# Decays in front of a token taken as a reciprocal, in place of a second scan

## The chip, the core and the metric

The kernel runs on one core of a Trainium2 chip. The metric is the device time of one execution in microseconds, as a median of several runs. A core has five engines with a queue of instructions each: PE (TensorE, matmuls), DVE (VectorE), ACT (ScalarE), POOL (GpSimd) and SP (which here only starts transfers). They run side by side and wait for each other through semaphores.

## What is computed

A linear recurrence with decays (RWKV-6 attention) and, on its output, a mixture of 16 experts. For each of 4 batches and 8 heads, over 768 tokens of 48 channels:

```
state = 0                                   # 48 x 48
for t in range(768):
    y[t]  = r[t] @ (state + outer(u * k[t], v[t]))
    state = w[t][:, None] * state + outer(k[t], v[t])
x = y, with the heads of a token side by side        # 3072 x 384
g = argmax(x @ w_group);  e = argmax(x @ w_expert[g])
out = weight(g, e) * relu(x @ w1[g, e]) @ w2[g, e]   # F = 1024
```

The decays w lie between 0.8 and 0.95.

## The kernel before

It has two stages. In the first, the recurrence is worked out in blocks of 64 tokens (`C`); two heads form a pair, which fills the 128 partitions (48 channels each, padded to 64), and there are 16 pairs. In the second, the tokens of each expert are gathered and sent through its two weight matrices.

**Blocks.** Within a block, a state that comes in is multiplied by the decays up to a token, and what a token leaves behind is multiplied by the decays after it. So the kernel scales keys and queries once and does the rest by matmuls:

- `s` (line 323, in `suffixes`) holds for every token the product of its own decay and all later ones of its block. It is a scan on DVE, run backward over a row of 780: each block has 65 places, the first of which holds a decay of zero. A second operand, `first_of`, holds 1 at these places and `FLOOR` elsewhere; the scan takes the larger of the product and this operand, so that every block starts anew from 1 and no product falls below `FLOOR`.
- `kk` (line 328, POOL) is the keys times the decays after their token, which is `s` shifted by one place.
- `total` is the product over a whole block: 12 numbers in a partition.
- `e` (lines 342 to 347, `prefixes`) holds what a query is multiplied by: the decays from the beginning of the block up to just before its token, divided by `total`. DVE makes 12 reciprocals of `total` (line 344), puts them at the first places of the blocks in a tile `iv` that is zero elsewhere, and runs a second scan forward: at a block's first place the decay is zero and the reciprocal enters by addition, and from there on each place is the one before it times its decay.
- `q` (line 351, `queries`, DVE) is the queries times `e`.

The product of `q` and `kk` of two tokens in one block is then the product of the decays between them, since `total` cancels. `masked` takes these scores on PE (line 366), keeps the pairs in order of time (line 376, DVE), and puts the diagonal from a second set of scores (line 380, DVE). `growth` (line 402, PE) makes what each block adds to the state, `states` (line 412, DVE) carries the state from block to block by a scan, and `outer` (line 447, PE) applies it to `q`.

**Order of the work.** The order on PE, DVE, ACT and SP is written out by hand: each engine runs its instructions in the order in which the code calls for them. One call of `step(n)` serves pair n and prepares the next two. On DVE it gives, in this order: masking and diagonal of pair n (lines 376, 380); `prefixes` and `queries` of pair n+1; the carry scan of pair n (line 412); the backward scan of pair n+2 (line 323). Once in a batch the routing of a batch comes between them (lines 140 to 170 and 502 to 528), some fifteen small operations; line 170 there is a reciprocal of 6 elements. Before the first step, `suffixes`, `prefixes` and `queries` of pair 0 and `suffixes` of pair 1 are called alone. Some loads (lines 191 and 206 to 217) and some stores are issued only after a named operation, so that transfers don't crowd: among these operations are the results of `prefixes` and `queries`.

`s`, `iv` and the carry tiles have two buffers each, used in turn; `e` has one. The zeros in `iv` are set once, by DVE for one buffer (line 250) and by POOL for the other (line 301).

**Second stage.** For each of the 16 experts PE makes the hidden layer (line 852) and the output (lines 887 and 907), with small work on ACT and DVE, while the weights of the expert after next are loaded. The loads for the first two experts are cut into pieces and issued during the first stage.

If a decay lies outside 0.5 to 2.0, a slow loop over tokens computes everything anew at the end; with the inputs here it isn't run.

Of the kernel before, what the change touches and what calls it, by code (L numbers as in the profile page):

```python
# [35 lines left out]
F32 = mybir.dt.float32  # L36
# [3 lines left out]
ALU = mybir.AluOpType  # L40
# [4 lines left out]
C = 64  # L45
# [3 lines left out]
CAP = max(CAPS)  # L49
LOW, HIGH = 0.5, 2.0  # L50

FLOOR = 1e-30
AFTER = mybir.DependencyInfo(mybir.DependencyClass.Sync, mybir.DependencyReason.DATA)


# [1 line left out]
def rwkv_then_moe(  # L57
# [12 lines left out]
    nc = tc.nc  # L70
    B, HP, _, _, S = rk_d.shape
# [3 lines left out]
    WP = w_d.shape[3]  # L75
# [96 lines left out]
    with ExitStack() as first:  # L172
        ip = first.enter_context(tc.tile_pool(name="inputs", bufs=1))
# [24 lines left out]
        def load_pair(n, after=None):  # L198
            load(rks[n % NRK], rk_d[n // HP, n % HP], after)
# [26 lines left out]


        ss = [ip.tile([128, WP + 1], F32, name=f"s{i}", tag=f"s{i}") for i in range(2)]
        ivs = [ip.tile([128, WP], F32, name=f"iv{i}", tag=f"iv{i}") for i in range(2)]
        tots = [ip.tile([128, D, NB], F32, name=f"tot{i}", tag=f"tot{i}") for i in range(2)]  # L230
        gs = [ip.tile([128, D, NB], F32, name=f"g{i}", tag=f"g{i}") for i in range(2)]
        first_of = ip.tile([128, WP], F32, name="first_of", tag="first_of")
# [10 lines left out]
        nc.scalar.dma_start(out=u_sb, in_=u_d)  # L243
        nc.vector.memset(first_of, FLOOR)
        nc.vector.memset(first_of[:, 0:WP:C + 1], 1.0)
# [1 line left out]
        load_values(0)  # L247
        make_identity(nc, ident)
        load_pair(1)
        nc.vector.memset(ivs[0], 0.0)  # L250
        nc.scalar.dma_start(out=wr, in_=wp_d)
        make_upper_triangular(nc, ut, val=1.0, diag=False)

# [44 lines left out]
        id_i = const([128, NE], I32, "id_i")  # L298

        def rest_of_setup():  # L300
            nc.gpsimd.memset(ivs[1], 0.0)
            nc.gpsimd.memset(blank, 0.0)
            nc.gpsimd.memset(blank[:, DM:DM + 1].bitcast(I32), N)
            nc.gpsimd.memset(within, 1.0)
            nc.gpsimd.memset(within[:, :, 0:1], 0.0)
            nc.gpsimd.memset(ones, 1.0)
            nc.gpsimd.tensor_scalar(out=order[:, 0:SPLIT], in0=order[:, 0:SPLIT],
                                    scalar1=float(2 ** 20), scalar2=None, op0=ALU.add)
            for p in range(NE):
                if p == 0 or CAPS[p] != CAPS[p - 1]:  # L310
                    nc.gpsimd.memset(caps[:, p:], float(CAPS[p]))
# [5 lines left out]
        def blocked(a):  # L317
            return a.rearrange("p (n c) -> p n c", c=C)

        def suffixes(n):  # L320
            p = dict(n=n, hp=n % HP, rk=rks[n % NRK], w=ws[n % NW], v=vts[n % NV],
                     s=ss[n % 2], iv=ivs[n % 2], tot=tots[n % 2], g=gs[n % 2])
            p["scanned"] = nc.vector.tensor_tensor_scan(out=p["s"][:, 0:WP][:, ::-1], data0=p["w"][:, ::-1],  # L323
                                         data1=first_of[:, ::-1], initial=1.0,
                                         op0=ALU.mult, op1=ALU.max)
            p["total"] = p["s"][:, 0:WP].rearrange("p (n c) -> p n c", c=C + 1)[:, :, 1]
            kk = p["kk"] = p2.tile([128, S], F32, name="kk", tag="kk")
            p["made"] = nc.gpsimd.tensor_tensor(  # L328
                out=blocked(kk), in0=blocked(p["rk"][:, 1]), op=ALU.mult,
                in1=p["s"][:, 1:].rearrange("p (n c) -> p n c", c=C + 1)[:, :, 1:])  # L330
            return p
# [8 lines left out]
                           in_=p["total"][:, None, 1:].to_broadcast([128, D, NB - 1]))  # L340

        def prefixes(p):
            iv = p["iv"][:, 0:WP:C + 1]
            nc.vector.reciprocal(out=iv, in_=p["total"])
            p["e"] = p2.tile([128, WP], F32, name="e", tag="e", bufs=1)
            return nc.vector.tensor_tensor_scan(out=p["e"], data0=p["w"], data1=p["iv"], initial=0.0,  # L346
                                         op0=ALU.mult, op1=ALU.add)

        def queries(p):
            p["q"] = p2.tile([128, S], F32, name="q", tag="q", bufs=3)  # L350
            return nc.vector.tensor_tensor(
                out=blocked(p["q"]), in0=blocked(p["rk"][:, 0]), op=ALU.mult,
                in1=p["e"].rearrange("p (n c) -> p n c", c=C + 1)[:, :, 0:C])

        blocks = [(c, j, slice(C * (2 * c + j), C * (2 * c + j + 1)))
                  for c in range(NCH) for j in range(2)]
# [195 lines left out]
        for e in range(2):  # L552
            w1, w2 = weights[e] = expert_weights()
            for w, w_in in ((w1, w1_d[e]), (w2, w2_d[e])):
                w = w.rearrange("p c f -> p (c f)")
                q = w.shape[1] // 4
# [15 lines left out]
        def step(n):  # L572
# [21 lines left out]
            if z:  # L594
                loads.send(prefixes(z))
                at = queries(z)
# [26 lines left out]
            if n + 2 < TOTAL:  # L623
                pipe[n + 2] = suffixes(n + 2)
                at = pipe[n + 2]["scanned"]
# [4 lines left out]
        def outputs(n, p, y, b):  # L630
# [13 lines left out]
            if half == 1:  # L644
                turning.append((b, lgs.pop(b), xs[b]))

        p = pipe[0] = suffixes(0)
        scaled(p)
        prefixes(p)
        queries(p)  # L650
        with tc.issue_after(p["made"].ins):
            rest_of_setup()
        keys(p)
        totals(p)
        pipe[1] = suffixes(1)
        load_decays(2, pipe[1]["scanned"])
        load_pair(2, pipe[1]["scanned"])
# [44 lines left out]
        def in_order():  # L702
# [33 lines left out]
        n = TOTAL  # L736
        nc.vector.scalar_tensor_tensor(
            out=seen[:, 0:SPLIT], in0=base_of[:, 0:SPLIT], scalar=128.0, in1=seen[:, 0:SPLIT],
            op0=ALU.add, op1=ALU.max)
        early = [early_tile(e, first_slots(e), copy)  # L740
                 for e, copy in enumerate((nc.scalar.copy, nc.vector.tensor_copy))]
        y, p = pipe[n - 2], pipe[n - 1]
# [359 lines left out]
    with tc.If(n_any, preferred_fallthrough_block=False):  # L1102
        n_over = nc.values_load(count_i[0:1, 0:1], min_val=0, max_val=OVT,
                                skip_runtime_bounds_check_because="a count of the tiles in use")
        with tc.For_i(0, n_over) as i:
# [7 lines left out]
                              in_=w1_d[ds(ev, 1)].rearrange("o p f -> p (o f)"))  # L1113
            nc.sync.dma_start(out=w2.rearrange("p c d -> p (c d)"),
                              in_=w2_d[ds(ev, 1)].rearrange("o p f -> p (o f)"))
# [9 lines left out]
                out=xg, out_offset=None, in_=slot_dram,  # L1125
# [64 lines left out]
```

## Time and profile before

| | |
|---|---|
| median of 3 runs | 472.78 us (466.01 to 473.24) |
| profiled execution | span 464.2 us |
| busy: PE, DVE, ACT, POOL | 415.1, 217.3, 159.9, 121.2 us |
| first stage: last masking of scores begins | 153.2 us |
| second scan, line 346 | 16 times, 1783 ns each |
| backward scan, line 323 | 16 times, 1763 ns each |
| 12 reciprocals, line 344 | 16 times, 214 ns each |
| product for the queries, line 351 | 16 times, 1039 ns each |
| keys on POOL, line 328 | 16 times, 1776 ns each |

In a row of a group, the form is written as output and input (partitions x elements and type); after the count stand busy time and the mean of one in ns, then the idle time of the engine in front of it and what ended it. In a timeline, each line has start and duration in us, and in brackets the idle time before it with the releaser. In a table of windows, each line has the length of the stretch and each engine's busy time in it, with the number of instructions; the last three numbers are the clock granted to TensorE as a share of full speed, the share of time in which the transfer engines were busy, and GB/s. "issue" as a releaser means that the engine waited for nothing that the profile shows.

### The profile page before, as it was taken

The page shows a single profiled execution, that of the slowest core. Times are in us where ns is not written, and L with a number is a line of the kernel's source. Part 1 is how long each engine was busy: PE and PEld are TensorE (multiplying, and loading weights), DVE is VectorE, ACT ScalarE, POOL GpSimd, SP SyncE. Part 2 cuts the span into 40 slices and gives each one's busy share as a digit, 9 for nine tenths or more (in the row PEclk, how much of TensorE's full clock was granted, in tenths as well). Part 3 has the DMA queues.
Part 4 walks back from the last instruction along what each step waited for, and adds up shares of the span by engine and source line. Part 5 has one row for each costly group of instructions (what it writes and reads, how often), then busy time and mean ns, then how long its engine had stood idle before and what let it go on. Part 6 is the DMA issues. An engine that isn't in the chain of part 4 may idle for free. (4 is left out here: it accounts for less than half of the span.)

```text
span 464.2 us, 15159 instructions
## 1 busy us (share of the span) xinstructions
PE 415.1 (89%) x6682; PEld 351.3 (76%) x6682; DVE 217.3 (47%) x326; ACT 159.9 (34%) x372; POOL 121.2 (26%) x136
## 2 busy tenths in 40 slices
PE   1786878877787989999999999999999999999995
PEld 1775767657666778799798797897987977877882
DVE  8898889969997434115363462511111111111111
ACT  3675867746575622122031120220211211210220
POOL 6312111560281523211211320213130221221011
PEclk9998999989898979999999999999999999999999
DMA  6769666784783523587779879766665667675400
GB/s 236 262 174 280 192 202 182 232 310 134 236 279 122 165 70 111 186 298 258 279 236 349 317 280 356 264 218 213 214 243 215 198 243 256 215 275 201 155 24 25
DMA packets 28537, 101.03 MB, mean 218 GB/s; under 512 B 4071, under 2 KB 11332, under 8 KB 24880
## 3 DMA queue, kind: packets, MB, share of 16 engines
q1 hardware_dynamic: 23344, 86.13, 55.7%
q0 software_dynamic: 4832, 13.79, 8.0%
q8 instruction: 54, 0.88, 0.8%
q14 instruction: 19, 0.16, 0.1%
q10 hardware_dynamic: 288, 0.07, 0.1%
HBM read 85.50 MB, written 14.75 MB: 216 GB/s over the span
## 5 line engine op out<-in xcount | busy, mean ns | idle before, releaser
L852 PE MATMUL bank_a<-xt,w 128*128 128x208 f32 (+5 forms) x768 | 128.6, 327 | 0.9 <-DVE xt L865 0.9
L852 PEld LDWEIGHTS bank_a<-xt,w 128*128 128x128 f32 x768 | 124.0, 190 | 4.1 <-issue 3.0
L887 PE MATMUL bank_b<-w,ht 128*128 128x384 f32 x224 | 75.5, 490 | 0.0
L882 DVE TENSOR_SCALAR yo<-bank_b,xg 128x384 f32<-128x384 f32 (+5 forms) x30 | 16.1, 538 | 117.5 <-PE bank_b L887 64.6
L854 ACT ACTIVATE ht<-bank_a 128x208 f32<-128x208 f32 (+5 forms) x128 | 41.6, 326 | 80.5 <-PE bank_a L852 79.9
L887 PEld LDWEIGHTS bank_b<-w,ht 128*128 128x128 f32 x224 | 41.4, 190 | 26.5
L875 POOL DMA_INDIRECT out_dram<-yo,xg x30 | 28.8, 959 | 120.4 <-DVE yo L882 102.8
L907 PEld LDWEIGHTS bank_b<-w,ht 128*32 128x32 f32 (+1 forms) x1344 | 50.3, 107 | 9.9 <-issue 7.3
L907 PE MATMUL bank_b<-w,ht 128*32 128x96 f32 (+3 forms) x1344 | 57.2, 324 | 0.0
L114 POOL DMA_INDIRECT slot_scratch<-blank,behind x28 | 26.5, 946 | 100.9 <-DMA slot_scratch<-blank,behind 61.1
L328 POOL TENSOR_TENSOR kk<-rk,s 128x768 f32<-128x768 f32 x16 | 28.4, 1776 | 86.6 <-DVE s L323 34.0
L447 PE MATMUL y<-q,zs 64*48 64x64 f32 x704 | 27.9, 229 | 20.5 <-issue 16.6
L865 DVE COPY xt<-bank_b 128x384 f32<-128x384 f32 (+5 forms) x30 | 12.8, 464 | 70.6 <-PE bank_b L863 70.6
L447 PEld LDWEIGHTS y<-q,zs 64*48 64x48 f32 x704 | 24.4, 129 | 22.6 <-issue 18.4
L916 ACT COPY yo<-bank_b 32x96 f32<-32x96 f32 (+1 forms) x30 | 7.0, 232 | 90.7 <-DVE yo L882 90.5
L536 POOL DMA_INDIRECT slot_scratch<-x,dest x24 | 29.7, 1236 | 26.5 <-ACT q L688 10.8
L346 DVE TENSOR_TENSOR_SCAN e<-w,iv 128x780 f32<-128x780 f32 x16 | 28.5, 1783 | 0.5
L323 DVE TENSOR_TENSOR_SCAN s<-w,first_of 128x780 f32<-128x780 f32 x16 | 28.2, 1763 | 0.9 <-DMA w<-in_w_dram 0.9
L389 PE MATMUL bank<-ident,kk 128*128 128x128 f32 x96 | 16.3, 311 | 11.8 <-POOL kk L328 10.5
L421 ACT COPY zs<-ze 128x576 f32<-128x576 f32 x16 | 19.8, 1238 | 9.5 <-DVE ze L412 9.2
L455 ACT COPY xt<-y 128x768 f32<-128x768 f32 x16 | 12.8, 799 | 28.8 <-PE y L447 28.8
L389 PEld LDWEIGHTS bank<-ident,kk 128*128 128x128 f32 x96 | 11.8, 157 | 13.5 <-POOL kk L328 11.1
(170 smaller groups left out, 477.2 us busy)
## 6 DMA issues: line engine op xcount, KB each, us to landing
w<-in_w_dram SPq DMA_DIRECT2D x28, 1536.0 KB, 7.3
rk<-in_rk_dram SPq DMA_DIRECT2D x26, 384.0 KB, 4.2
wt<-in_w_dram SPq DMA_DIRECT2D x4, 1560.0 KB, 8.5
w<-in_w_dram SPq DMA_DIRECT2D x16, 384.0 KB, 4.3
w<-in_w_dram SPq DMA_DIRECT2D x26, 195.0 KB, 3.4
v<-in_v_dram SPq DMA_DIRECT2D x16, 288.0 KB, 4.3
xg<-slot_scratch SPq DMA_DIRECT2D x14, 193.0 KB, 6.2
rk<-in_rk_dram SPq DMA_DIRECT2D x3, 768.0 KB, 7.5
```

The costliest lines, as they stand in the source:

```text
L114: nc.gpsimd.indirect_dma_start(out=slot_dram, in_=blank[0:m], in_offset=None, out_offset=bass.IndirectOffsetOnAxis(ap=behind[0:m, p, i:i + ...
L323: p["scanned"] = nc.vector.tensor_tensor_scan(out=p["s"][:, 0:WP][:, ::-1], data0=p["w"][:, ::-1], data1=first_of[:, ::-1], initial=1.0, o ...
L328: p["made"] = nc.gpsimd.tensor_tensor(out=blocked(kk), in0=blocked(p["rk"][:, 1]), op=ALU.mult, in1=p["s"][:, 1:].rearrange("p (n c) -> p ...
L346: return nc.vector.tensor_tensor_scan(out=p["e"], data0=p["w"], data1=p["iv"], initial=0.0, op0=ALU.mult, op1=ALU.add)
L389: nc.tensor.transpose(b[:, c * 128:(c + 1) * 128], z[:, (c0 + c) * 128:(c0 + c + 1) * 128], ident)
L447: m = nc.tensor.matmul(p["y"][j][64 * t:64 * t + D, C * c:C * (c + 1)], lhsT=p["zs"][halves[t], i], rhs=p["q"][halves[t], C * i:C * (i + 1 ...
L536: m = nc.gpsimd.indirect_dma_start(out=slot_dram, out_offset=bass.IndirectOffsetOnAxis(ap=dest[:, c:c + 1], axis=0), in_=x[:, c, :], in_of ...
L852: nc.tensor.matmul(z[:, 0:n], lhsT=w1[:, dc, f * 128:(f + 1) * 128], rhs=xt[:, dc], start=(dc == 0), stop=(dc == DC - 1))
L854: nc.scalar.activation(out=ht[:, f, 0:n], in_=z[:, 0:n], func=AF.Relu)
L875: s = out_scatter[0] = nc.gpsimd.indirect_dma_start(out=out, out_offset=bass.IndirectOffsetOnAxis(ap=to, axis=0), in_=yo[0:m], in_offset=N ...
L887: nc.tensor.matmul(z[0:m, 0:DM], lhsT=ht[:, f, 0:m], rhs=w2[:, f], start=(f == 0), stop=(f == FC - 1))
L907: nc.tensor.matmul(z[32 * i:32 * i + k, c:c + b - a], lhsT=lhs, rhs=w2[:, f, a:b], start=(f == 0 and c == 0), stop=(f == FC - 1), skip_gro ...
```

## The change

The product of the decays up to just before a token, divided by the product over the whole block, is one over the product of the token's own decay and all later ones. That is what the backward scan holds at this token: with places counted as in a block of 65, `e[i] = 1 / s[i+1]`. So the change takes the reciprocal of `s` at all 64 tokens of each of the 12 blocks, 768 in a partition, and needs neither the second scan nor `iv`. It is meant to put one plain operation on DVE in place of a scan and a small operation. `e` loses the gaps between blocks in the part that is used, so that the product for the queries reads rows without gaps.

`FLOOR` goes from 1e-30 to 1e-20. It bounds the products from below, and so the reciprocals from above.

```diff
-FLOOR = 1e-30
+FLOOR = 1e-20
...
-        ivs = [ip.tile([128, WP], F32, name=f"iv{i}", tag=f"iv{i}") for i in range(2)]
...
-        nc.vector.memset(ivs[0], 0.0)
...
         def rest_of_setup():
-            nc.gpsimd.memset(ivs[1], 0.0)
...
         def prefixes(p):
-            iv = p["iv"][:, 0:WP:C + 1]
-            nc.vector.reciprocal(out=iv, in_=p["total"])
             p["e"] = p2.tile([128, WP], F32, name="e", tag="e", bufs=1)
-            return nc.vector.tensor_tensor_scan(out=p["e"], data0=p["w"], data1=p["iv"], initial=0.0,
-                                         op0=ALU.mult, op1=ALU.add)
+            return nc.vector.reciprocal(
+                out=blocked(p["e"][:, 0:S]),
+                in_=p["s"][:, 0:WP].rearrange("p (n c) -> p n c", c=C + 1)[:, :, 1:])
 
         def queries(p):
             p["q"] = p2.tile([128, S], F32, name="q", tag="q", bufs=3)
             return nc.vector.tensor_tensor(
-                out=blocked(p["q"]), in0=blocked(p["rk"][:, 0]), op=ALU.mult,
-                in1=p["e"].rearrange("p (n c) -> p n c", c=C + 1)[:, :, 0:C])
+                out=p["q"], in0=p["rk"][:, 0], in1=p["e"][:, 0:S], op=ALU.mult)
```

More of the change, by code (lines that the diff above doesn't have):

```diff
@@ L321, in suffixes @@
             p = dict(n=n, hp=n % HP, rk=rks[n % NRK], w=ws[n % NW], v=vts[n % NV],
-                     s=ss[n % 2], iv=ivs[n % 2], tot=tots[n % 2], g=gs[n % 2])
+                     s=ss[n % 2], tot=tots[n % 2], g=gs[n % 2])
             p["scanned"] = nc.vector.tensor_tensor_scan(out=p["s"][:, 0:WP][:, ::-1], data0=p["w"][:, ::-1],
```

## The prediction

> **What bounds the kernel now.** I read four views, from coarse to fine. First the page's busy shares and its 40 slices of 11.6 us, here the PE and DVE rows:
>
> ```profile
> PE 415.1 (89%) x6682; PEld 351.3 (76%) x6682; DVE 217.3 (47%) x326; ACT 159.9 (34%) x372; POOL 121.2 (26%) x136
> PE   1786878877787989999999999999999999999995
> DVE  8898889969997434115363462511111111111111
> ```
>
> The 89% of PE is an average over two stages. In the first 13 slices (to about 150 us) VectorE is mostly at 8 to 9 tenths and PE, after the first slice, at 6 to 8; later PE is at 9. The change lies wholly in the first stage, so PE's 89% says nothing on it.
>
> Second, the timeline of VectorE over one step of the first stage (start us, us, line):
>
> ```profile
> 36.62 0.93 DVE L376 TENSOR_TENSOR at<-scores,later 128x768 f32<-128x768 f32 x1
> 37.66 1.03 DVE L380 COPY_PREDICATED at<-diag_mask,scores 128x768 f32<-128x768 uint8 x1
> 38.58 0.22 DVE L344 RECIPROCAL iv<-s 128x12 f32<-128x12 f32 x1
> 38.84 1.78 DVE L346 TENSOR_TENSOR_SCAN e<-w,iv 128x780 f32<-128x780 f32 x1
> 40.65 0.96 DVE L351 TENSOR_TENSOR q<-rk,e 128x768 f32<-128x768 f32 x1
> 41.53 1.35 DVE L412 TENSOR_TENSOR_SCAN ze<-g,tot 128x576 f32<-128x576 f32 x1
> 42.80 1.75 DVE L323 TENSOR_TENSOR_SCAN s<-w,first_of 128x780 f32<-128x780 f32 x1
> 47.03 0.96 DVE L376 TENSOR_TENSOR at<-scores,later 128x768 f32<-128x768 f32 x1 [2.48 <-PE scores L366]
> ```
>
> The seven operations run back to back, 7.9 us from 36.62 to 44.55; only then does VectorE wait, 2.48 us, for PE's scores. Other steps have no bracket at L376: they begin at 20.95, 28.79 and 36.62, a period of 7.83 us that is VectorE's work alone. Third, all such waits:
>
> ```profile
> DVE at L376 <- PE scores L366: 11.2, 7, 3.9
> ```
>
> In 16 steps VectorE waits 11.2 us: 0.64, 2.48, 0.49, 1.26, 3.91, 1.86 and 0.59 by the timeline; nine steps have none. Fourth, two steps by windows (span, then PE, PEld, DVE, ACT, POOL):
>
> ```profile
> 28.79:36.62 7.83, 5.65 (x206) 4.82 (x205) 7.66 (x8) 5.91 (x11) 1.69 (x1) 1.00 0.62 155
> 36.62:47.03 10.41, 7.11 (x223) 6.10 (x216) 7.76 (x9) 5.20 (x10) 3.38 (x2) 0.84 0.94 295
> ```
>
> VectorE is busy 7.66 of 7.83 us in the first: it bounds the step. In the second its work is the same, and PE is late (granted clock 0.84, DMA share 0.94).
>
> [...]the trace of before has no large reciprocal. [...]the product q of 768 elements took 958 ns[...].
>
> **The change part by part.** *Reciprocal over 768 elements.* The two small reciprocals, and a neighbour of the same size (lines of the source view: min/median/max in ns):
>
> ```profile
> L170 DVE RECIPROCAL x<-es x4: 192/193/194, 80.9 to 167.3; 128x6 f32<-128x6 f32 x4
> L344 DVE RECIPROCAL iv<-s x16: 205/214/231, 6.2 to 146.2; 128x12 f32<-128x12 f32 x16
> L168 DVE SCALAR_TENSOR_TENSOR es<-sums,es x4: 165/166/167, 80.7 to 167.1; 128x6 f32<-128x6 f32 x4
> ```
>
> Six elements cost 193 ns as a reciprocal and 166 as another operation. For twelve I take the 231 ns: that is the instance at 6.21 us, which like L170 waits for the operation before it, while the other fifteen start under the tail of their predecessor, and such starts shorten a record (the scan at L323: 1758 against 1783). Then (231 - 193)/6 = 6.3 ns an element[...], and 193 - 6 x 6.3 = 155 ns fixed[...]. [...]For 768 elements: 155 + 768 x 6.25 = 4.96 us. Bounds: [...]the rate of q, gives 0.96 us[...]. I take 4.96. The weakness is an extrapolation from 12 to 768 elements, with a strided input in the one case and a strided output in both.
>
> *Removed.* In a step, the small reciprocal and the scan: from 38.58 to the start of q at 40.65 is 2.07 us. In their place stand 4.96 us and the same 0.04 us gap in front of q. Net: 4.96 + 0.04 - 2.07 = +2.93 us on VectorE in each of the 15 steps that prepare a pair, and once ahead of the loop.
>
> *What is queued behind it.* q, the carry scan (L412), the scan of the pair after next (L323) and the next masking all start 2.93 us later. PE needs q for the next scores, but then has the carry scan and L323 (3.0 us) in hand, so no new wait arises: 48 matmuls took 0.93 us. Loads whose issue is tied to L346 and L351 come later within a step that is longer by as much.
>
> *What is absorbed.* Where VectorE waits for PE now, PE's queue is late for its own reasons, and later VectorE work fits into the wait: 2.48 + 0.49 + 1.26 + 2.93 (of 3.91) + 1.86 + 0.59 = 9.6 us. The nine steps without a wait absorb nothing.
>
> *Ahead of the loop.* There q took 2.25 us beside POOL's kk (3.10 us). The reciprocal would run from 6.21 to 11.17, after kk's end (9.72 us), so q takes 0.96 and ends at 12.17, 1.6 us later than the 10.54 of now. PE was busy with transposes until 11.24, so first scores, and the first masking, move by about 1.0 us.
>
> *At nothing.* The product with a dense operand: 768 elements either way[...]. The memset on VectorE (0.71 us) lies in front of a wait for the first load (0.90 us before L323), the one on POOL (0.74 us) behind kk with nothing urgent after it. The floor is a constant in a tile. PE, ACT and the stage of experts keep their instructions; the second stage begins when the first ends, so the delay reaches the end whole.
>
> *Sum:* 15 x 2.93 = 44.0, minus 9.6, plus 1.0 = +35.4 us: 472.8 + 35.4 = 508.2.
>
> **The rivals.**
> - [...]A step falls by 2.07 - 1.00 = 1.07 us. Only the nine steps without a wait can gain, at most 9.6 us, and PE, busy 5.7 to 7.1 us in such a step with idle spots of 1 to 3 us ("issue") that VectorE doesn't cause, would stop part of it. Half: 472.8 - 4.8 = 468.[...]
>
> **How the numbers follow.** Forecast 0.66 (slower, 508)[...]. The time is the forecast's. [...]Slower by over 2% (above 482): [...]0.81. Within 2%: most of the fast rival, 0.14. Faster by over 2% needs 9.5 us, all that the fast rival could give: 0.05.
>
> **What would show it.** After the change, the row of the reciprocal with 768 elements: 4.96 us if the rate is right. The period of an undisturbed step: 10.8 us, with VectorE above 0.95 of it and brackets at L376 nearly gone (one, of about 1 us, where 3.91 stood). The PE row of the first stage falls, the experts' stage keeps its length. The forecast is wrong if the reciprocal takes 1 to 2 us; if it takes 5 us and the steps grow by much less than 2.9, the wrong step is what I call absorbed.

## The result and the profile after

The changed kernel takes 500.65 us (median of three, 500.0 to 501.19) where the kernel before took 472.78 us: it is slower, by a ratio of 1.0665 (95% interval 1.048 to 1.085). In a second comparison the medians were 502.24 and 475.74 us, a ratio of 1.0537 (1.0477 to 1.0596). Executions of one kernel can fall into a slower state; the ratios leave those out, so that they aren't the quotients of these medians. The profiled executions have spans of 498.2 and 464.2 us.

The page of the kernel after, busy shares and the slices of PE and VectorE (a slice is now 12.5 us):

```profile
PE 429.7 (86%) x6682; PEld 365.5 (73%) x6682; DVE 261.6 (52%) x309; ACT 160.5 (32%) x372; POOL 112.7 (23%) x135
PE   1766886678577867999999999999999999999995
DVE  7999999999999994231266156251110111110111
```

VectorE's row now reads 9 from the second slice to the end of the first stage, and its busy time grew by 44.3 us with 17 instructions fewer. The costliest new row of the groups, with count, busy time and mean:

```profile
L341 DVE RECIPROCAL e<-s 128x768 f32<-128x768 f32 x16 | 79.0, 4936 | 0.0
```

One reciprocal of 768 elements takes 4.94 us. It stands in the place of a scan and a small reciprocal that took 2.0 us together. The timeline of VectorE over one step, after:

```profile
46.61 0.93 DVE L371 TENSOR_TENSOR at<-scores,later 128x768 f32<-128x768 f32 x1
47.64 1.02 DVE L375 COPY_PREDICATED at<-diag_mask,scores 128x768 f32<-128x768 uint8 x1
48.55 4.94 DVE L341 RECIPROCAL e<-s 128x768 f32<-128x768 f32 x1
53.52 0.96 DVE L347 TENSOR_TENSOR q<-rk,e 128x768 f32<-128x768 f32 x1
54.40 1.35 DVE L407 TENSOR_TENSOR_SCAN ze<-g,tot 128x576 f32<-128x576 f32 x1
55.67 1.76 DVE L320 TENSOR_TENSOR_SCAN s<-w,first_of 128x780 f32<-128x780 f32 x1
57.34 0.93 DVE L371 TENSOR_TENSOR at<-scores,later 128x768 f32<-128x768 f32 x1
```

A step is 10.73 us, all of it VectorE's, which is busy for 10.59 of it, and nothing stands in brackets at the second L371. In the views of waits, of VectorE for PE and of PE for VectorE:

```profile
PE scores L361 <- DVE q L347: 24.1, 12, 3.1
DVE at L375 <- PE scores L361: 0.3, 1, 0.3
```

The 11.2 us that VectorE waited at the masking are gone; the 0.3 us at the diagonal stood there before too. In their place PE waits for the product q, up to 3.1 us in a step. By windows, two steps in a row, after (span, then PE, PEld, DVE, ACT, POOL, granted clock, DMA share, GB/s):

```profile
35.87:46.61 10.74, 6.48 (x252) 5.59 (x248) 10.60 (x8) 5.91 (x11) 1.67 (x1) 1.00 0.48 143
46.61:57.34 10.73, 7.99 (x250) 6.93 (x248) 10.59 (x7) 6.22 (x11) 1.68 (x1) 0.84 0.67 201
```

The second step had a granted clock of 0.84, the first 1.00, and they last 10.73 and 10.74 us: in these steps TensorE's clock doesn't decide the time.

Cut at the last masking (line 376 before, 371 after) and at the routing's end, where the order of experts is written (line 724 before, 719 after), the two executions part like this:

| | first stage | routing of the last batch, first tiles | experts | span |
|---|---|---|---|---|
| before | 153.18 | 31.66 | 279.36 | 464.20 us |
| after | 186.76 | 32.14 | 279.30 | 498.20 us |

The whole difference but half a microsecond lies in the first stage.

### The profile page after: what moved, and what is told of

The parts are those of the page before. It is cut to its first block, busy times and chain, and to the rows that moved or that the text cites. A ratio compares the mean times of both kernels' runs of the same rounds, so it can differ in the third digit from the quotient of the medians.

```text
span 498.2 us, 15142 instructions
## 1 busy us (share of the span) xinstructions
PE 429.7 (86%) x6682; PEld 365.5 (73%) x6682; DVE 261.6 (52%) x309; ACT 160.5 (32%) x372; POOL 112.7 (23%) x135
## 5 line engine op out<-in xcount | busy, mean ns | idle before, releaser
L341 DVE RECIPROCAL e<-s 128x768 f32<-128x768 f32 x16 | 79.0, 4936 | 0.0
L325 POOL TENSOR_TENSOR kk<-rk,s 128x768 f32<-128x768 f32 x16 | 26.8, 1677 | 128.5 <-DVE s L320 63.9
L361 PE MATMUL scores<-q,kk 64*64 64x64 f32 x768 | 18.3, 253 | 24.1 <-DVE q L347 24.1
L361 PEld LDWEIGHTS scores<-q,kk 64*64 64x64 f32 x768 | 15.7, 162 | 27.2 <-DVE q L347 26.7
L442 PEld LDWEIGHTS y<-q,zs 64*48 64x48 f32 x704 | 25.7, 136 | 10.3 <-issue 6.8
L531 POOL DMA_INDIRECT slot_scratch<-x,dest x24 | 24.5, 1023 | 27.3 <-DVE dest L523 10.8
L384 PE MATMUL bank<-ident,kk 128*128 128x128 f32 x96 | 17.6, 330 | 11.5 <-POOL kk L325 10.3
```

Source lines behind the costliest of these rows:

```text
L325: p["made"] = nc.gpsimd.tensor_tensor(out=blocked(kk), in0=blocked(p["rk"][:, 1]), op=ALU.mult, in1=p["s"][:, 1:].rearrange("p (n c) -> p ...
L341: return nc.vector.reciprocal(out=blocked(p["e"][:, 0:S]), in_=p["s"][:, 0:WP].rearrange("p (n c) -> p n c", c=C + 1)[:, :, 1:])
L361: nc.tensor.matmul(z[halves[j], 512 * t + C * c:512 * t + C * (c + 1)], lhsT=lhs[hs, sl], rhs=rhs[hs, sl], start=True, stop=True)
L442: m = nc.tensor.matmul(p["y"][j][64 * t:64 * t + D, C * c:C * (c + 1)], lhsT=p["zs"][halves[t], i], rhs=p["q"][halves[t], C * i:C * (i + 1 ...
L531: m = nc.gpsimd.indirect_dma_start(out=slot_dram, out_offset=bass.IndirectOffsetOnAxis(ap=dest[:, c:c + 1], axis=0), in_=x[:, c, :], in_of ...
```

## The experiments

**The price of a reciprocal.** The theory: a reciprocal on VectorE costs some 6.2 ns an element. The rival: it is the gaps in what the change reads, not the operation. A price list was put into the second stage of the kernel before:

```diff
+        if part == 0:
+            for n in (96, 192, 384, 768):
+                nc.vector.reciprocal(out=p_to[:, 0:n], in_=pz[:, 0:n])
+        if part == 1:
+            nc.vector.reciprocal(out=p_to[:, 0:768].rearrange("p (n c) -> p n c", c=64),
+                                 in_=pz.rearrange("p (n c) -> p n c", c=65)[:, :, 1:])
+            nc.vector.reciprocal(out=p_to[:, 0:96], in_=pz[:, 0:768:8])
+        if part == 2:
+            nc.scalar.activation(out=p_to[:, 0:768], in_=pz[:, 0:768], func=AF.Ln)
+            nc.scalar.activation(out=p_to[:, 0:768], in_=p_to[:, 0:768], func=AF.Exp, scale=-1.0)
```

> The kernel before, with a price list in the second stage, where VectorE and ScalarE have spare time; its results aren't used. Reciprocals of 96, 192, 384 and 768 dense elements, one of 768 read with the gaps of the change, one of 96 read at every eighth place, and a logarithm and an exponential of 768 elements on ScalarE. If a reciprocal costs a rate of some 6.2 ns an element on top of 0.155 us: 0.75, 1.35, 2.55 and 4.94 us, the one with gaps 4.94, the one at every eighth place 0.75. If it is the gaps that make the reciprocal of the change slow, and not the operation: the dense one of 768 near 1 us, and the 4.94 only with gaps. The logarithm and the exponential should take 0.93 us each, as the scaled copy of the queries does, with or without a table load in front.

The groups of this kernel, shapes kept apart:

```profile
L1071 DVE RECIPROCAL p_to<-pz 128x768 f32<-128x768 f32 x1 | 5.0, 4953 | 0.0
L1073 DVE RECIPROCAL p_to<-pz 128x768 f32<-128x768 f32 x1 | 4.9, 4941 | 0.0
...
L1071 DVE RECIPROCAL p_to<-pz 128x384 f32<-128x384 f32 x1 | 2.6, 2553 | 0.0
L1071 DVE RECIPROCAL p_to<-pz 128x192 f32<-128x192 f32 x1 | 1.4, 1354 | 0.0
...
L1075 DVE RECIPROCAL p_to<-pz 128x96 f32<-128x96 f32 x1 | 0.8, 754 | 0.0
L1071 DVE RECIPROCAL p_to<-pz 128x96 f32<-128x96 f32 x1 | 0.7, 742 | 0.0
```

The two records of 96 elements differ by 12 ns, as do those of 768. From the longer one of each, the slope is (4953 - 754)/672 = 6.25 ns, on top of 154 ns. The points between lie on it: 1354 and 2553 ns. With gaps (L1073) it costs no more than dense, 4941 ns against 4953, and 96 elements at every eighth place (L1075) take 754 ns against 742 dense. The rival is out. The logarithm and the exponential took 0.84 us each, but began 2.2 us apart (397.6 and 399.8 us), so that some 1.4 us lie between them; the one table load in the profile of before (line 263) takes 1.28 us. If each of the two operations draws such a load, they would cost ScalarE 4.2 us in a step by these durations, an estimate, on top of the 5.9 us that it is busy in a step of 7.83 us before; that way was not built in.

**The same VectorE time of another kind.** The theory: the reciprocal harms by its length alone. The rival: it also disturbs other engines, since in the trace after the granted clock of the first stage fell from 0.96 to 0.88. So nearly the same time was added to the kernel before as a scan and a product, into a tile that is overwritten afterwards:

```diff
         def prefixes(p):
+            p["e"] = p2.tile([128, WP], F32, name="e", tag="e", bufs=1)
+            nc.vector.tensor_tensor_scan(out=p["e"], data0=p["w"], data1=first_of, initial=1.0,
+                                         op0=ALU.mult, op1=ALU.max)
+            nc.vector.tensor_tensor(out=p["e"][:, 0:S], in0=p["w"][:, 0:S], in1=p["s"][:, 0:S],
+                                    op=ALU.mult)
             iv = p["iv"][:, 0:WP:C + 1]
```

> The kernel before, with a scan of 780 and a product of 768 added on VectorE in front of the 12 reciprocals; their results are overwritten. That adds about 1.82 + 1.00 us, nearly what the change adds (2.91 us in a step), without a long reciprocal. If only VectorE's time counts: an undisturbed step of 10.7 us in place of 7.83, and the same time as the changed kernel, within 3 us. If the long reciprocal does harm besides its length[...]: clearly faster than the changed kernel, by 5 us or more.

It took 497.5 us (496.29 to 499.75; ratio to before 1.0587, 1.05 to 1.0674). VectorE in one step of it:

```profile
48.65 1.77 DVE L344 TENSOR_TENSOR_SCAN e<-w,first_of 128x780 f32<-128x780 f32 x1
50.45 0.96 DVE L346 TENSOR_TENSOR e<-w,s 128x768 f32<-128x768 f32 x1
51.33 0.22 DVE L349 RECIPROCAL iv<-s 128x12 f32<-128x12 f32 x1
```

The added work moved the small reciprocal from 48.65 to 51.33, by 2.68 us, and undisturbed steps are 10.52 us: 0.22 less than with the long reciprocal, over 16 steps 3.5 us. The last masking begins at 184.29 against 186.76 us, and the span is 496.1 against 498.2: 2.5 and 2.1 us less, not more than VectorE's shorter work explains. So the time is that of VectorE's length, and no loss is left for the rival. The granted clock over the whole execution was 0.939 here, 0.943 after the change and 0.976 before: as low as after the change, without a long reciprocal in it; what lowers it wasn't looked into.

**A smaller addition,** the product alone:

```diff
+            nc.vector.tensor_tensor(out=p["e"][:, 0:S], in0=p["w"][:, 0:S], in1=p["s"][:, 0:S],
+                                    op=ALU.mult)
```

> The kernel before, with only the product of 768 added on VectorE in each step; its result is overwritten. It adds about 1.0 us. If steps with a wait absorb as much as they wait, and the nine without absorb nothing: 15 x 1.0, minus 1.0 + 0.49 + 1.0 + 1.0 + 1.0 + 0.59, plus up to 1 ahead of the loop: +10 to +11 us. If PE's slack hides a microsecond in a step: below +3. If nothing is absorbed: +16.

An undisturbed step grew to 8.70 us, by 0.87. The median was 475.15 us (471.95 to 479.17) beside 469.91 of before on the same chip: ratio 1.0112 (1.0083 to 1.0141), some 5 us. That is half of what was expected: 15 x 0.87 is 13 us, of which some 8 were absorbed and not 5. And its profile still shows 7.5 us of waits at the same place:

```profile
DVE at L378 <- PE scores L368: 7.5, 5, 3.9
```

Waits of before that the addition should have filled stand there again, in part at other steps. So the waits of one trace aren't a fixed stock that is filled up; this is taken up below.

**The cost doubled,** each long reciprocal made twice:

```diff
+            again = p2.tile([128, S], F32, name="again", tag="again", bufs=1)
+            nc.vector.reciprocal(
+                out=blocked(again),
+                in_=p["s"][:, 0:WP].rearrange("p (n c) -> p n c", c=C + 1)[:, :, 1:])
```

> The changed kernel with each long reciprocal made twice, the first one into a tile that nobody reads. If the first stage of the changed kernel is VectorE's work alone, with no wait left, each of the 16 adds its whole 4.97 us: +79.5 us on the changed kernel, about 580 us, with steps of 15.7 us. If other engines still had a part in it: less, by what they had.

It took 576.53 us (576.08 to 578.03). In a step (the last line is the next masking):

```profile
49.66 0.93 DVE L375 TENSOR_TENSOR at<-scores,later 128x768 f32<-128x768 f32 x1
...
51.63 4.92 DVE L342 RECIPROCAL again<-s 128x768 f32<-128x768 f32 x1
56.48 4.88 DVE L345 RECIPROCAL e<-s 128x768 f32<-128x768 f32 x1
...
65.22 0.93 DVE L375 TENSOR_TENSOR at<-scores,later 128x768 f32<-128x768 f32 x1
```

A step is 15.55 us, 4.81 more than after; 15 of them and 4.16 us ahead of the loop are 76.3 us, and the spans differ by 574.6 - 498.2 = 76.4. Nothing was absorbed: in the changed kernel no slack is left on VectorE. (4.81 and not 4.97: the second of two reciprocals starts at 56.48, while the record of the first runs to 56.55, and takes 4.88 us.)

**Less work on VectorE.** If VectorE bounds the first stage, taking work off the kernel before should help until PE takes over. The product for the queries was given to POOL:

```diff
-            return nc.vector.tensor_tensor(
+            return nc.gpsimd.tensor_tensor(
                 out=blocked(p["q"]), in0=blocked(p["rk"][:, 0]), op=ALU.mult,
```

> The kernel before, with the product for the queries (L351, 0.96 us) moved from VectorE to POOL, where the like product kk takes 1.7 us. An undisturbed step of VectorE falls from 7.83 to 6.95 us. If VectorE alone bounded the first stage: 15 x 0.88, some 13 us less than before. If PE takes over, as the share of 5.7 to 7.7 us that it is busy in a step lets expect: VectorE's waits for scores grow by as much as it saves, and the time falls by 0 to 5 us. If the product on POOL, which the scores need at once, stands behind kk or a transfer's issue on POOL: slower than before.

It was slower: 481.52 us against 475.74 (ratio 1.0129, 1.0095 to 1.0164). The third outcome holds, for its reason in part and for one that wasn't expected. In the source view of this kernel (min/median/max in ns) the backward scan on VectorE and the product on POOL, and both in one step, with the carry scan in front:

```profile
L323 DVE TENSOR_TENSOR_SCAN s<-w,first_of x16: 1751/2487/3210, 4.2 to 152.1; 128x780 f32<-128x780 f32 x16
L351 POOL TENSOR_TENSOR q<-rk,e x16: 1670/2402/2641, 10.1 to 162.1; 128x768 f32<-128x768 f32 x16
...
44.56 1.33 DVE L412 TENSOR_TENSOR_SCAN ze<-g,tot 128x576 f32<-128x576 f32 x1
44.78 2.60 POOL L351 TENSOR_TENSOR q<-rk,e 128x768 f32<-128x768 f32 x1 [2.18 <-PE y L447]
45.81 3.21 DVE L323 TENSOR_TENSOR_SCAN s<-w,first_of 128x780 f32<-128x780 f32 x1
```

Where the two run side by side, the scan takes up to 3.21 us in place of 1.76 and the product up to 2.64 in place of 1.67. The product ends 1.49 us after the carry scan (47.38 against 45.89), and the backward scan 1.64 us after the product (49.02); in the two steps that follow, whose scans start at 54.15 and 65.03, it is 1.64 us again. These times fit a reading in which the one that starts later waits for the other to end, rather than both being slowed all along; what makes it wait was not shown. So VectorE is spared 0.88 us in a step and loses up to 1.45, and its busy time in the first stage is 137.9 us where it was 135.6. The keys' product on POOL mostly escapes it in the kernels before and after: it runs beside the masking and the diagonal and takes 1.67 to 1.71 us. Only the first one of before met a scan and q, and took 3.10.

The expected reason, q behind other work on POOL, fits other steps. In the step from 89.77 to 99.27 us POOL was busy for 8.37 us in six instructions, where in the one from 40.59 to 48.94 it was busy for 4.29 in two. The factor `e` was ready at 93.82 us, and VectorE waited for the scores until 99.27:

```profile
99.27 0.96 DVE L376 TENSOR_TENSOR at<-scores,later 128x768 f32<-128x768 f32 x1 [2.53 <-PE scores L366]
```

How the loss divides between the two was not separated. VectorE's waits in this first stage, 22.3 us in all, lie near the longest that executions of before show below.

**The reciprocals on POOL,** as powers with an exponent of -1:

```diff
-            return nc.vector.reciprocal(
-                out=blocked(p["e"][:, 0:S]),
-                in_=p["s"][:, 0:WP].rearrange("p (n c) -> p n c", c=C + 1)[:, :, 1:])
+            return nc.gpsimd.tensor_tensor(
+                out=blocked(p["e"][:, 0:S]), op=ALU.pow,
+                in0=p["s"][:, 0:WP].rearrange("p (n c) -> p n c", c=C + 1)[:, :, 1:],
+                in1=minus[:, None, :].to_broadcast([128, NB, C]))
```

> The changed kernel, with the reciprocals of the 768 elements taken on POOL, as powers with an exponent of -1, in place of VectorE. VectorE's step falls to about 5.8 us of work. POOL has some 6 us free in a step. If a power of 768 elements takes at most 5 us there: a little faster than the kernel before, with PE as the bound. If it takes 10 us or more, POOL bounds the first stage, and the time grows by 15 times what goes beyond about 6 us.

```profile
L343 POOL TENSOR_TENSOR e<-s,minus 128x768 f32<-128x768 f32 x16 | 1964.9, 122803 | 0.1
```

One of them takes 122.8 us, 160 ns an element, and the kernel 2406 us. That is no way out.

**How far executions lie apart.** The small addition had shown that the waits of one trace can't be counted on. The changed kernel again, with more executions of before beside it, and then the kernel before for two more profiles:

> The changed kernel as it is, beside the kernel before on one chip, to compare how far single executions of the two lie apart. If the first stage of the changed kernel is VectorE's work without a wait, what varies in PE's queue has no place in it: its times should lie within 2 to 3 us, and those of before within some 9 us as seen so far.

> The kernel before as it is, for another profile of it: its times lay between 466 and 480 us, and the profile that the forecast was worked out from was of an execution of 466. If the spread is VectorE's waits for PE's scores in the first stage: an execution of 470 us or more shows waits of more than 11.2 us at L376, more by about what it takes longer, and undisturbed steps of 7.83 us still. If it lies in the experts' stage: 11 us of waits again, and a later second stage of other length.

> The same kernel once more, with the same two expectations: a time 5 us over 466 should come with 5 us more of waits in the first stage, or, if the spread lies in the experts' stage, with 11 us of waits as in the first profile.

The four times of the changed kernel lay within 2.0 us (501.21 to 503.22), the 21 of before within 8.6 (470.95 to 479.53); four of course spread less than 21, so the profiles have to show it. The two new profiles of before are of executions of 480.41 and 474.33 us. Cut as above:

| execution | first stage | routing, first tiles | experts | span |
|---|---|---|---|---|
| before, the profile of the forecast | 153.18 | 31.66 | 279.36 | 464.20 us |
| before, second new profile | 158.59 | 34.31 | 279.70 | 472.60 us |
| before, first new profile | 163.39 | 32.84 | 282.37 | 478.60 us |
| after, the profile shown | 186.76 | 32.14 | 279.30 | 498.20 us |
| after, the later profile | 186.73 | 31.09 | 281.98 | 499.80 us |

Most of the spread of before, 5.4 of 8.4 and 10.2 of 14.4 us, lies in the first stage. VectorE's waits there, up to the last masking, in the view of waits of the second new profile and then of the first ("remote" stands for a releaser that the view doesn't name):

```profile
DVE at L376 <- PE scores L366: 13.0, 9, 3.3
DVE at L376 <- remote: 1.7, 1, 1.7
DVE ze L412 <- ACT g L407: 1.0, 1, 1.0
...
DVE before L516 <- PE scores L511: 0.8, 1, 0.8
...
DVE at L380 <- PE scores L366: 0.3, 1, 0.3
```

```profile
DVE at L376 <- PE scores L366: 13.7, 9, 3.1
DVE at L380 <- remote: 3.6, 1, 3.6
DVE at L376 <- remote: 3.2, 1, 3.2
...
DVE before L516 <- PE scores L511: 0.8, 1, 0.8
...
DVE at L380 <- PE scores L366: 0.3, 1, 0.3
```

These are 16.8 and 21.6 us where the forecast's profile has 11.5 (11.2 and 0.3 at the diagonal): 5.3 and 10.1 us more, and the first stages are longer by 5.4 and 10.2. So the first stages of before differ by what VectorE waits; 6.8 of the 21.6 us and 1.7 of the 16.8 are for the releaser that isn't named. The two new executions ran on the same chip, so that chips alone don't make the difference. After the change these waits all but vanish (0.3 us, and 0.9 in the later profile): in two profiles of separate executions the last masking begins at 186.76 and 186.73 us. The second expectation, a spread in the experts' stage, holds only for 3.0 of the 14.4 us of one of them.

## Why the prediction was right, and which term was mis-sized

The forecast was slower, 508.2 us; measured were 500.65. Direction and cause hold; the sum was 7.5 us too high.

- *The rate of the reciprocal.* Forecast 6.25 ns an element on 155 ns, 4.96 us; measured 4.94 in place, 6.25 ns on 154 ns in the price list. Two records of 6 and 12 elements gave the rate, because the record with the same kind of start was taken (231 ns); with the median of 214 ns the slope would have come out at 3.5 ns. That the rate was met so closely owes something to luck: the working gave 6.3 ns, and one ns more or less in one of the two records moves it by 0.17. The rate of q, 0.96 us for 768 elements, is out. That the 155 ns are a fixed cost was an estimate; they lie near the 166 ns that another operation on six elements took.
- *The step.* Forecast +2.93 us and 10.8 us; measured +2.91 (10.74 against 7.83), with VectorE busy for 0.99 of it. That q is late makes PE wait, but adds no wait on VectorE, as the forecast said.
- *Ahead of the loop.* Forecast +1.0; the first masking moved from 12.87 to 14.15, +1.28, and to 13.45 in the later profile, +0.58. But the first scan, which waits for a load, began at 4.39 us before and at 4.70 and 4.00 after. Taken from its start, the masking moved by 0.97 us in both. Right.
- *At nothing.* Experts' stage 279.30 against 279.36 us; the removed memset only lengthened the wait for the load. Right.
- *What is absorbed: the mis-sized term.* Between the two profiles it comes out near: 15 x 2.91 + 1.28 - 33.58 (the growth of the first stage) = 11.4 us absorbed, forecast 9.6. The larger part of the difference is the wait of 3.91 us, of which the forecast let only 2.93 be filled: that step even became shorter, from 11.82 to 10.74. A reading that fits is that PE's late spots now fall into time in which PE waits anyway; no run tests it. But the profile was of an execution of 465.98 us, and its +35.4 us were set on a median of 472.78. An execution that takes longer has more waits in the first stage (16.8 and 21.6 us in the new profiles, where this one had 11.5), and a step of 10.74 us swallows those too. Profile on profile the change costs 34.0 us of span; median on median 27.9, which means that 43.7 + 1.3 + 0.5 - 27.9 = 17.6 us of the sum are missing. Not all of them need be absorbed waits: in the two new profiles about two thirds of what they take longer lies in the first stage, the rest behind it, and the execution of 472.78 us has no profile. Had the forecast been set on the time of the execution that it was read from, 466.0 + 35.4 = 501.4, it would have met the measured time within a microsecond. The new profiles bear this out: with the first stage of each brought to the 186.7 us of after, and the rest as it is, 474.33 becomes 502.5 and 480.41 becomes 503.8 us, near the 500.0 to 503.2 that the changed kernel took in all its runs.

Why the scores come late by another amount each time isn't settled. In the first stage of the two new profiles of before the granted clock was 0.91 and PE was busy for 122 us, in the forecast's profile 0.96 and 113 us, which goes with it; no run here set the clock.

What would beat both kernels was not found. The two attempts to take work off VectorE with POOL were slower: the product saved VectorE nothing and came later for PE, and the power has too low a rate.

## What to carry to other kernels

Before an operation is swapped for another "of the same size", look for it in the trace at any size: two small records of one operation, taken where they start in the same way, give a rate and a fixed cost, to be checked at full size; here the line from 6 and 12 elements (6.3 ns and 155 ns) held up to 768 (4.94 us). A change that is counted from one trace belongs on the time of that execution, not on a median of others: where another engine's lateness varies, as here, the longer executions hold the waits that slower work will fill. And an operation that is moved to an engine with time to spare needs a look at what runs beside it and in front of it there, not only at that engine's share.

## What the runs showed of the hardware beyond this

- A reciprocal on VectorE costs 6.25 ns an element on top of 154 ns, dense or with gaps, from 96 to 768 elements (4953 ns). A scan costs some 2.0 ns an element, an estimate from the medians of two scans of before: 1758 ns for 780 (line 323) and 1350 for 576 (line 412).
- A power on POOL took 122.8 us for 768 elements, 160 ns each.
- The backward scan on VectorE beside the product for the queries on POOL: up to 3.21 in place of 1.76 us, and up to 2.64 in place of 1.67; in the three instances above, the later one ends 1.64 us after the product (the scan) and, in the first of them, 1.49 us after the carry scan (the product).
- A logarithm and an exponential right after it on ScalarE took 0.84 us each and began 2.2 us apart, with more time between them than one of them takes.
